# Up projection of two token groups as seven products of half sums, with the first query tiles moved into the key/value stage

## The chip, the cores and the metric

The kernel runs on one core of a Trainium2 chip. Times are device microseconds of one execution on that core. A core has TensorE (PE) for matrix products into PSUM, VectorE (DVE), ScalarE (ACT) and GpSimd (POOL) for work on the elements, and SyncE (SP), which here only issues DMAs. Each engine takes its own instructions strictly in the order in which the program lists them; semaphores make one engine wait for another.

## The reference

One block of a model over 2048 tokens of width 512. After a layernorm, two branches read the same normalised `xn`, and their outputs are added to `x`:

```python
qkv = (x @ wqkv)...                      # 32 heads of 16
pq = einsum("bhsd,hdf->bhsf", q, w_phi); pk = ... k
phi = concat([softmax(p), softmax(-p)])  # 32 features a head
kv = einsum("bhsf,bhsd->bhfd", phi_k, v);  z = sum over s of phi_k
o = (phi_q @ kv) / (phi_q @ z + 1e-6);     A = o @ wo
g = xn @ w_gate;  u = xn @ w_up            # 512 x 1792
B = (g * u) @ w_down
return x + A + B
```

Inputs and output are bf16. The branch B is called the FF branch here; its 1792 columns are 14 "FF tiles" of 128.

## The kernel before

**Layout.** Tokens are 16 tiles of 128, and four groups of 512 (`sg` 0 to 3). `xnT` holds the transposed normalised tokens as four 128-row parts `q`. FF results `h = g*u` lie transposed in `hT`, f16, one 128-row tile for each `ft`.

**How the order comes about.** The code records steps (`sc.step`, `sc.dma`) in a written order, with the memory each step reads and writes; `_record` (line 101) derives the dependencies, for PSUM by whole banks of 512 f32 columns. `_plan` (line 199) then orders the steps on each engine by estimated costs: among the steps that are ready within a small window, the one recorded first goes first. `sc.chain` adds order by hand. The emitted program has a fixed order for each engine and a semaphore wait for every dependency not already known to be met. In `_record`, before the change, a step that overwrites what the same engine (ACT or DVE) only reads needs no wait.

**Stages.**
- Start: ten `warm` products, layernorm of tiles 0 to 3 on DVE, their transposes on PE (`T`, line 597), and FF tiles 0 to 3 for group 0 in small pieces (`U1`, `U2`). An ACT or DVE step copies each transposed tile out of PSUM.
- K/V stage (loop at line 957), once for each token tile: `LN` for later tiles, `K(t)` (line 659), `V(t)` (line 669), and `KV(t)` (line 685), which accumulates in banks 6 and 7. `features` (line 640) makes the projection folded with `w_phi`, two exponentials on ACT, and a reduction (1024 to 64) on DVE; a reciprocal of the sums on DVE follows, then `even_up` on POOL (a ratio and a product of 512 elements). `LN` hands a normalised tile to a DMA transpose on SP. `FOLD` makes the folded weights. Between these, FF units `U(ft, sg)` (line 708) are strewn in: four gate matmuls of 512 columns, copied by ACT into a ring of four slots, four up matmuls, and on DVE the product of both. PSUM tiles of K, V and the FF units come from a ring of six banks.
- Down stage (loop at line 999), in eight pairs of token tiles: `Q(t)` (line 746, like K, then a DMA transpose of `phi_q`), `NUM(t)` (line 764: products with `kv`, division, DMA transpose into `oT`), the down projection, and the FF units left over (line 935 to 937: group 1 and 2 in `U`, group 3 in `U2` of 256 columns). Four banks are left to the ring; banks 4 and 5 serve the down projection.

**The seven products of the down projection.** `DOWN_STEPS` (line 838) already computes each 2 by 2 block product (two token tiles by two column halves, with the 14 FF tiles as two halves of seven) as seven products instead of eight. `TSUMS` and `SSUMS` (lines 804 and 813) make the half sums on POOL; partial results are added in PSUM or by DVE.

Names used below: `nm` is the normalised tile, `xe` the eviction of a transposed tile, `ge`/`ke`/`qe` the ACT evictions of gate, K and Q tiles, `fe` those of the fold, `kr`/`qr` the DVE reductions, `kc`/`qc` the reciprocals, `vs`/`vz` the two steps that scale V by the reciprocal (DVE) and copy the reciprocal (ACT), `h` the DVE product of gate and up, `gu` an FF unit that has both in one bank.

Of the kernel before, what the change touches and what calls it, by code (L numbers as in the profile page):

```python
# [6 lines left out]
F16 = mybir.dt.float16  # L7
# [13 lines left out]
NT = S_TOK // 128  # L21
# [66 lines left out]
class _Sched:  # L88
# [12 lines left out]
    def _record(self, st, reads, writes):  # L101
        deps = []

        def spans(ap):
            space = str(ap.tensor.name)
            ivs = _ap_intervals(ap)
            if space == "ps":
                ivs = sorted(set((b * 2048, b * 2048 + 2048)
                                 for lo, hi in ivs for b in range(lo // 2048, (hi + 2047) // 2048)))
            return space, ivs  # L110

        for ap in reads:
            space, ivs = spans(ap)
            for lo, hi in ivs:
                regs = self._overlaps(space, lo, hi)
                for reg in regs:
                    for w in reg[2]:
                        if w is not st:
                            deps.append(w)
                    if space == "ps":  # L120
                        for r in reg[3]:
                            if r.eng != st.eng:
                                deps.append(r)
                    reg[3].append(st)
                if not regs:
                    raise RuntimeError(f"step {st.idx} ({st.eng} {st.name}) reads unwritten {space}[{lo}:{hi}]")
        for ap in writes:
            space, ivs = spans(ap)
            for lo, hi in ivs:
                new_regions = []  # L130
                for reg in self._overlaps(space, lo, hi):
                    for w in reg[2]:
                        if w is not st:
                            deps.append(w)
                    for r in reg[3]:
                        if r is not st and not (r.eng == st.eng and st.eng in (ACT, DVE)):
                            deps.append(r)
                    if reg[0] < lo:
                        new_regions.append([reg[0], lo, list(reg[2]), list(reg[3])])
                    if reg[1] > hi:  # L140
                        new_regions.append([hi, reg[1], list(reg[2]), list(reg[3])])
                    self.regions[space].remove(reg)
                self.regions[space].extend(new_regions)
                self.regions[space].append([lo, hi, [st], []])
        seen = set()
        dd = []
        for d in deps:
            if id(d) not in seen:
                seen.add(id(d))
                dd.append(d)  # L150
        st.deps = dd
# [192 lines left out]
        _build(nc, es, A_x, A_wqkv, A_w_phi, A_wo, B_w_gate, B_w_up, B_w_down, out)  # L344


def _build(nc, es, A_x, A_wqkv, A_w_phi, A_wo, B_w_gate, B_w_up, B_w_down, out):
    layout = {}
    cur = [0]

    def alloc(name, nelem_bf16):
        off = (cur[0] + 31) // 32 * 32
        layout[name] = off
        cur[0] = off + nelem_bf16
        return off
# [17 lines left out]
    alloc("mask68", 68)  # L373
    alloc("vext", 4 * 8 * 68)
    alloc("E", NE * 1024)
    alloc("qT", NQT * 1024)
    alloc("kvbd", 8 * 68)
    alloc("oring", 3 * 512)
    alloc("oT", 4 * 512)
    alloc("gring", 4 * 512)  # L380
    alloc("hT", NF * 1536)
    alloc("Tw", 3 * 7 * 256)
    alloc("tf", 2 * 2 * 3 * 256)
    alloc("ostg", 4 * 512)
    alloc("stats", 2 * NT * 6)
    alloc("mv", 2 * NT * 2)
    alloc("rstd", 2 * NT)
# [56 lines left out]
    def mm_cost(n):  # L444
        return max(25.0, n / 2.4 + 2.5)

    def mm(items, name=""):
        def fn(e):
            ins = None
            for (o, l, r, s, p) in items:  # L450
                ins = e.matmul(o, lhsT=l, rhs=r, start=s, stop=p, skip_group_check=True)  # L451
            return ins
        reads, writes, c = [], [], 0.0
        for o, l, r, s, p in items:
            reads += [l, r]
            writes.append(o)
            c += mm_cost(o.free_size())
        st = sc.step(PE, fn, reads=reads, writes=writes, cost=c, name=name)
        st.ns = tuple(o.free_size() for o, _, _, _, _ in items)
        return st  # L460
# [159 lines left out]
    def FOLD(w):  # L620
        for dt in range(NQ):
            b = nb()
            mm([(bank(b, jt * 128, 128), wT_v[:, w, jt, dt * 128:(dt + 1) * 128], wbd_v[:, jt, :], True, True)
                for jt in range(NQ)], name=f"F{w}")
            act_op(Wp_v[:, w, dt, :], bank(b), name=f"fe{w}{dt}")

# [24 lines left out]
    def even_up(ev, sm, rc, ratio, name, t):  # L651
# [4 lines left out]
                                       in1=ratio[:, :, None].to_broadcast([128, H, 16]), op=ALU.mult),  # L656
             [ev[:, :, 1, :], ratio], [ev[:, :, 1, :]], 1030.0, name=f"{name}p{t}")

    def K(t):
        Et = Eslot(ectr[0])  # L660
        ectr[0] += 1
        Ek[t] = Et
        sm, rs, ratio = sums_v[:, t % 4, :], rs_v[:, t % 4, :], ratio_v[:, t % 4, :]
        ev = features(Et, 1, t, sm, "k")
        dve(lambda e: e.reciprocal(out=rs, in_=sm), [sm], [rs], cost=500.0, name=f"kc{t}")  # L665
        rv = rs.rearrange("p (h s) -> p h s", s=2)
        even_up(ev, sm, rv[:, :, 1], ratio, "k", t)

# [23 lines left out]
    def KVX():  # L692
        src = psum[:, 6 * 512:8 * 512].rearrange("p (c j) -> p c j", c=8)[:, :, 0:68]
        dve(lambda e: e.tensor_tensor(out=kvbd_v, in0=src, in1=mask68[:, None, :].to_broadcast([128, 8, 68]),
                                      op=ALU.mult), [src, mask68], [kvbd_v], cost=640.0, name="kvx")

    hT_v = sbv("hT", 0, NF * 1536).bitcast(F16).rearrange("p (f s) -> p f s", f=NF)

    def hs(s_lo):
# [8 lines left out]
    def U(ft, sg):  # L708
        bg, bu = nb(), nb()
        s_lo = sg * 512  # L710
        mm(group(bank(bg), [(wg_v[:, q, ft * 128:(ft + 1) * 128], xnT(q, s_lo, 512)) for q in range(NQ)]),
           name=f"g{ft}.{sg}")
        g = gring()
        act_op(g, bank(bg), name=f"ge{ft}.{sg}")
        mm(group(bank(bu), [(wu_v[:, q, ft * 128:(ft + 1) * 128], xnT(q, s_lo, 512)) for q in range(NQ)]),
           name=f"u{ft}.{sg}")
        h = hT_v[:, ft, hs(s_lo):hs(s_lo) + 512]
        dve(lambda e: e.tensor_tensor(out=h, in0=bank(bu), in1=g, op=ALU.mult), [bank(bu), g], [h],  # L718
            name=f"h{ft}.{sg}")

    def U2(ft, s_lo):
        b = nb()
# [23 lines left out]
    def Q(t):  # L746
# [3 lines left out]
        rc = qsm_v[:, t % 4, :]  # L750
        ev = features(Et, 0, t, sm, "q")
        smv = sm.rearrange("p (h s) -> p h s", s=2)
        dve(lambda e: e.reciprocal(out=rc, in_=smv[:, :, 1]), [sm], [rc], cost=270.0, name=f"qc{t}")  # L753
        even_up(ev, sm, rc, ratio, "q", t)
        sc.dma(SP, qT_v[:, t % NQT, :, :], Et, 262144, turn=True, reads=[Et], writes=[qT_v[:, t % NQT, :, :]],
               name=f"qT{t}")
# [33 lines left out]
    S_v = arena[:, so:so + 8 * HF * 128].bitcast(F16).rearrange("p (r w k s) -> p r w k s", r=2, w=4, k=HF)  # L790
    tf_v = sbf("tf", 0, 2 * 3 * 256).rearrange("p (r w j) -> p r w j", r=2, w=3)

    def parts(v):
        return [v[:, k, :] for k in range(v.shape[1])]

    def sums(eng, out_, a_, b_, op, name):
        fn = lambda e: e.tensor_tensor(out=out_, in0=a_, in1=b_, op=op)  # L797
        n = out_.free_size()
        if eng == POOL:
            pool(fn, parts(a_) + parts(b_), parts(out_), 100.0 + 2.0 * n, name=name)  # L800
        else:
            dve(fn, parts(a_) + parts(b_), parts(out_), cost=60.0 + 0.53 * n, name=name)

    def TSUMS():
        for n, (o_, a_, b_) in enumerate(((T1, B12, B11), (T2, B22, T1), (T4, B21, T2), (T3, B22, B12))):
            for lo, hi in ((0, 2), (2, 4), (4, 6), (6, HF)):
# [4 lines left out]
        return hT_v[:, half * HF:(half + 1) * HF, s:s + 128]  # L811

    def SSUMS(p):
        assert ui[0] >= done_by[p]
        S1, S2, S3, S4 = (S_v[:, p % 2, w] for w in range(4))
        A11, A12, A21, A22 = hA(0, 2 * p), hA(1, 2 * p), hA(0, 2 * p + 1), hA(1, 2 * p + 1)
        sums(POOL, S3, A11, A21, ALU.subtract, f"S3.{p}")
# [113 lines left out]
    U2(2, 256)  # L931
    U2(3, 256)
    sc.chain("st0 ag0 st1 ag1 nm0.0 nm0.1 nm1 xe1d st2 ag2 h0t0 st3 ag3 nm2 h1t0 nm3 xe2d xe3d h0t1")
    sc.chain("ln0 rs0 ln1 rs1 xe0a xe0b xe1a ge0t0 ln2 rs2 ge1t0 ln3 rs3 xe2a xe3a")
    units = [(U, ft, 0) for ft in range(4, NF)] + [(U, ft, sg) for sg in (1, 2) for ft in range(NF)]
    done_by = {0: 10, 1: 10, 2: 24, 3: 24, 4: 38, 5: 38, 6: 52, 7: 66}
    units += [(U2, ft, s_lo) for s_lo in (1536, 1792) for ft in range(NF)]
    ui = [0]

    def nextU():  # L940
        if ui[0] < len(units):
            u = units[ui[0]]
            u[0](*u[1:])
            ui[0] += 1

# [5 lines left out]
    nextU()  # L951
    LN([4, 5])
    LN([6, 7])
    NA = 30
    QL = 3
    load_wT(0)
    for t in range(NT):
        if t % 2 == 0 and t + 8 < NT:
            LN([t + 8, t + 9])
        K(t)  # L960
        nextU()
        if t >= 1:
            V(t - 1)
        while ui[0] < 3 + (t + 1) * (NA - 7) / NT:
            nextU()
        if t >= 3:
            KV(t - 3)
        if t == 8:
            FOLD(0)
    sc.dma(SP, wd_v, B_w_down.rearrange("(f p) j -> p f j", p=128), 1835008, writes=[wd_v], name="wd")  # L970
    load_sq(SP, wo_v, A_wo.rearrange("(q p) j -> p q j", p=128), 524288, "wo")
    sc.chain("x12 xT4 xT5 xT6 xT7 wT0 xT8 xT9 xT10 xT11 wd xT12 xT13 wo xT14 xT15")
    TSUMS()
    Q(0)
    V(NT - 1)
    KV(NT - 3)
    nextU()
    Q(1)
    KV(NT - 2)
    nextU()  # L980
    Q(2)
    KV(NT - 1)
    KVX()
    ring_banks[0] = [0, 1, 2, 3]
    rp[0] = 0
    SSUMS(0)
    down = DOWN_STEPS(0)
    nextU()
    Q(3)
    down[0]()  # L990
    down[1]()
    NUM(0)
    nextU()
    NUM(1)
    SSUMS(1)
    u0 = ui[0]
    n_left = len(units) - u0
    NP = NT // 2
    for p in range(NP):
# [29 lines left out]
        down[6]()  # L1029
        some(1.0)  # L1030
        down[7]()

    eng_sems = {e: es.enter_context(nc.semaphore(f"sem_{e}")) for e in (PE, ACT, DVE, POOL, SP)}
    dma_sems = [es.enter_context(nc.semaphore(f"dsem{i}")) for i in range(sc.dma_count)]
# [37 lines left out]
```

## Time and profile before

| | us |
|---|---|
| median of 5 runs (lowest to highest) | 217.81 (217.54 to 218.5) |
| the profiled execution | 217.76 |
| its span, first to last instruction | 215.9 |

The profile is a record of every instruction of one execution. Its page gives the busy time of each engine, the busy share in 40 equal slices of the span, the chain of work that ended last, and groups of instructions by source line. PE is the matmul part of TensorE and PEld its weight loads, which overlap the matmuls. Line 451 is the helper through which every matmul but the warm-up goes, and line 423 the one of most ACT steps, so groups there mix stages; the shapes tell them apart. The mean duration of a PE matmul [...] is longer than the distance from one matmul to the next. Busy shares over the whole span mix stages; the trace can also be asked for the busy time within a window, for what an engine waited for, and for the instructions in order of time.

POOL and DVE are the next busiest by the page, and their load differs by stage:

```profile
DVE  4766599986757756878893747766876588667663
ACT  4656988784464454445343232342142332331000
POOL 4020153459999998285835536839759568322540
```

### The profile page before, as it was taken

The page shows a single profiled execution, that of the slowest core. Times are in us where ns is not written, and L with a number is a line of the kernel's source. Part 1 is how long each engine was busy: PE and PEld are TensorE (multiplying, and loading weights), DVE is VectorE, ACT ScalarE, POOL GpSimd, SP SyncE. Part 2 cuts the span into 40 slices and gives each one's busy share as a digit, 9 for nine tenths or more (in the row PEclk, how much of TensorE's full clock was granted, in tenths as well). Part 3 has the DMA queues.
Part 4 walks back from the last instruction along what each step waited for, and adds up shares of the span by engine and source line. Part 5 has one row for each costly group of instructions (what it writes and reads, how often), then busy time and mean ns, then how long its engine had stood idle before and what let it go on. Part 6 is the DMA issues. An engine that isn't in the chain of part 4 may idle for free.

```text
span 215.9 us, 4165 instructions
## 1 busy us (share of the span) xinstructions
PE 210.6 (98%) x1632; PEld 140.5 (65%) x1654; DVE 152.3 (71%) x313; ACT 91.6 (42%) x204; POOL 123.2 (57%) x143
## 2 busy tenths in 40 slices
PE   8999999999999999999999999999999999999995
PEld 3775444444455444545556667888888889888984
DVE  4766599986757756878893747766876588667663
ACT  4656988784464454445343232342142332331000
POOL 4020153459999998285835536839759568322540
PEclk9999999999999999999999999999999999999999
DMA  5999796792000000003453132162433415434121
GB/s 167 325 262 362 202 105 120 221 290 52 0 0 0 3 0 0 3 0 58 88 102 73 49 76 46 53 100 56 68 73 72 92 34 101 98 73 99 47 78 51
DMA packets 48660, 19.96 MB, mean 92 GB/s; under 512 B 37376, under 2 KB 48640, under 8 KB 48640
## 3 DMA queue, kind: packets, MB, share of 16 engines
q1 hardware_dynamic: 47968, 19.36, 38.8%
q10 hardware_dynamic: 672, 0.33, 0.5%
q8 instruction: 13, 0.21, 0.4%
q14 instruction: 7, 0.06, 0.1%
HBM read 8.67 MB, written 2.10 MB: 50 GB/s over the span
## 4 chain that ended last, share of the span: by engine, by line
PE 93%; DMA 2%; SPq 1%; issue 1%; ACT 0%; DVE 0%; DVEq 0%
PE ps L451 93%; DMA arena<-in_B_w_up_dram 2%; SPq L173 1%; ACT arena L423 0%; DVE arena L729 0%; DVE arena L830 0%; DVEq L343 0%; DVE arena L893 0%
## 5 line engine op out<-in xcount | busy, mean ns | idle before, releaser
L451 PE MATMUL ps<-arena 128*128 128x256 bf16 (+4 forms) x1622 | 206.4, 288 | 2.0 <-DMA arena<-in_B_w_up_dram 0.4
L451 PEld LDWEIGHTS ps<-arena 128*128 128x128 bf16 (+1 forms) x1644 | 139.2, 98 | 69.8 <-DVE arena L583 0.9
L423 ACT ACTIVATE arena<-ps 128x512 bf16<-128x512 f32 (+2 forms) x155 | 75.6, 529 | 94.9 <-PE ps L451 94.4
L797 POOL TENSOR_TENSOR arena<-arena 128x896 f16<-128x896 f16 (+2 forms) x48 | 76.3, 1597 | 25.7 <-PE ps L451 16.9
L647 DVE TENSOR_REDUCE arena<-arena 128x64 f32<-128x1024 bf16 x32 | 38.9, 1217 | 23.6 <-ACT arena L423 23.4
L655 POOL TENSOR_TENSOR arena<-arena 128x512 bf16<-128x512 bf16 x32 | 33.7, 1054 | 1.6
L830 DVE TENSOR_TENSOR arena<-ps,arena 128x256 f32<-128x256 f32 (+1 forms) x56 | 23.2, 413 | 11.9 <-PE ps L451 11.8
L718 DVE TENSOR_TENSOR arena<-ps,arena 128x512 f16<-128x512 f32 x38 | 25.8, 678 | 7.5 <-PE ps L451 7.5
L653 POOL TENSOR_TENSOR arena<-arena 128x32 f32<-128x32 f32 x32 | 8.3, 259 | 32.5 <-DVE arena L753 18.7
L729 DVE TENSOR_TENSOR arena<-ps,arena 128x256 f16<-128x256 f32 x32 | 13.3, 414 | 12.0 <-ACT arena L423 12.0
L423 ACT ACTIVATE arena<-arena 128x2 f32<-128x2 f32 (+2 forms) x32 | 14.0, 457 | 3.6 <-POOL arena L573 2.2
L564 DVE BATCH_NORM_STATS2 arena<-arena 128x6 f32<-128x512 bf16 x16 | 10.5, 676 | 2.1 <-DMA arena<-in_A_x_dram 2.0
L573 POOL TENSOR_SCALAR arena<-arena 128x1 f32<-128x1 f32 x12 | 3.0, 266 | 15.1 <-ACT arena L423 15.1
L777 DVE TENSOR_TENSOR arena<-ps,arena 128x512 bf16<-128x512 f32 x16 | 11.0, 686 | 0.3
L676 DVE TENSOR_TENSOR arena<-ps,arena 128x512 bf16<-128x512 f32 x16 | 10.1, 632 | 0.6 <-PE ps L451 0.6
L665 DVE RECIPROCAL arena<-arena 128x64 f32<-128x64 f32 x16 | 8.7, 542 | 0.0
L679 ACT ACTIVATE arena<-arena 128x32 bf16<-128x32 f32 x16 | 3.7, 232 | 9.3 <-DVE arena L665 9.3
L546 POOL TENSOR_TENSOR arena<-arena 128x128 bf16<-128x128 bf16 x4 | 1.6, 424 | 8.8 <-DMA arena<-in_A_w_phi_dram 8.8
L773 DVE RECIPROCAL arena<-arena 128x32 f32<-128x32 f32 x16 | 5.6, 352 | 0.5
L753 DVE RECIPROCAL arena<-arena 128x32 f32<-128x32 f32 x16 | 5.5, 345 | 0.1
L907 PE MATMUL ps<-const-bfloat16-1.0 128*128 128x512 bf16 x10 | 4.4, 626 | 0.8 <-PEq L1057 0.8
L893 DVE TENSOR_TENSOR arena<-ps,arena 128x256 bf16<-128x256 f32 (+1 forms) x9 | 3.4, 385 | 0.0
(18 smaller groups left out, 16.8 us busy)
## 6 DMA issues: line engine op xcount, KB each, us to landing
arena<-in_B_w_down_dram SPq DMA_DIRECT2D x1, 1792.0 KB, 7.7
out_dram<-arena SPq DMA_DIRECT2D x14, 128.0 KB, 2.0
arena<-in_A_x_dram SPq DMA_DIRECT2D x3, 512.0 KB, 9.3
arena<-in_B_w_gate_dram SPq DMA_DIRECT2D x1, 768.0 KB, 8.0
arena<-in_B_w_up_dram SPq DMA_DIRECT2D x1, 768.0 KB, 8.4
arena<-arena SPq DMA_TRANSPOSE x44, 3.1
arena<-in_B_w_gate_dram SPq DMA_DIRECT2D x2, 256.0 KB, 4.6
arena<-in_B_w_gate_dram SPq DMA_DIRECT2D x1, 512.0 KB, 6.3
```

What stands on the lines that cost most here:

```text
L423: return e.activation(out=out_ap, in_=in_ap, func=func, scale=scale, **kw)
L451: ins = e.matmul(o, lhsT=l, rhs=r, start=s, stop=p, skip_group_check=True)
L564: dve(lambda e, t=t: e.bn_stats(stats_v[:, t, :], x_tile(t)), [x_tile(t)], [stats_v[:, t, :]], cost=560.0, name=f"st{t}", win=win)
L647: dve(lambda e: e.tensor_reduce(out=sm, in_=Et.rearrange("p (h f) -> p h f", f=16), axis=AX.X, op=ALU.add), [Et], [sm], cost=1130.0, name= ...
L655: pool(lambda e: e.tensor_tensor(out=ev[:, :, 1, :], in0=ev[:, :, 1, :], in1=ratio[:, :, None].to_broadcast([128, H, 16]), op=ALU.mult), [ ...
L665: dve(lambda e: e.reciprocal(out=rs, in_=sm), [sm], [rs], cost=500.0, name=f"kc{t}")
L676: dve(lambda e: e.tensor_tensor(out=o1, in0=src, in1=rp_[:, :, :, None].to_broadcast([128, 8, 4, 16]), op=ALU.mult), [src, rs_v[:, t % 4, ...
L718: dve(lambda e: e.tensor_tensor(out=h, in0=bank(bu), in1=g, op=ALU.mult), [bank(bu), g], [h], name=f"h{ft}.{sg}")
L729: dve(lambda e: e.tensor_tensor(out=h, in0=bank(b, 256, 256), in1=g, op=ALU.mult), [bank(b, 256, 256), g], [h], name=f"h{ft}.{s_lo}")
L777: dve(lambda e: e.tensor_tensor(out=ov, in0=src, in1=wv4[:, :, :, None].to_broadcast([128, 8, 4, 16]), op=ALU.mult), [src, w], [o], cost=6 ...
L797: fn = lambda e: e.tensor_tensor(out=out_, in0=a_, in1=b_, op=op)
L830: dve(lambda e: e.tensor_tensor(out=out_, in0=in_ps, in1=in_sb, op=ALU.add), [in_ps, in_sb], [out_], cost=328.0, name=f"{name}.{p}")
```

## The change

For FF tiles 0 to 5 and 7 to 12, the up projection of token groups 1 and 2 becomes seven products. A block takes the 2 by 2 arrangement of FF tiles `ft` and `ft+7` by token groups 1 and 2, with the 512-wide contraction as two halves of 256. Each product is two matmuls of 512 columns. `XSUMS` makes four half sums of `xnT` once, on DVE (eight steps of 128x512); `WSUMS` makes four half sums of `w_up` for each block, on POOL (steps of 128x256). Both are f16. Tiles 6 and 13 keep the old unit. Gate products keep their four matmuls, as units `G` of their own.

```diff
+    def XSUMS(eng):
+        X1, X2, X3, X4 = (Tx_v[:, w] for w in range(4))
+        for n, (o_, a_, b_) in enumerate(((X1, xB(0, 2), xB(0, 1)), (X3, xB(1, 2), xB(0, 2)), (X2, xB(1, 2), X1),
+                                          (X4, xB(1, 1), X2))):
+            for k in range(2):
+                sums(eng, o_[:, k:k + 1], a_[:, k:k + 1], b_[:, k:k + 1], ALU.subtract, f"Xs{n}.{k}")
...
+    def WSUMS(ft):
+        S1, S2, S3, S4 = (Su_v[:, ft % NSW, w] for w in range(4))
+        A = lambda i, k: wA(wu_v, i, k, ft)
+        sums(POOL, S3, A(0, 0), A(1, 0), ALU.subtract, f"w3.{ft}")
+        sums(POOL, S1, A(1, 0), A(1, 1), ALU.add, f"w1.{ft}")
+        sums(POOL, S2, S1, A(0, 0), ALU.subtract, f"w2.{ft}")
+        sums(POOL, S4, A(0, 1), S2, ALU.subtract, f"w4.{ft}")
...
+    def BLOCK(ft, banks):
...
+        def p1():
+            xprod(pa, A(0, 0), xB(0, 1), True, f"b1.{ft}")
+            st["c"] = bank(nb())
+            seed(st["c"], pa, f"sd.{ft}")
+
+        def p7():
+            xprod(pb, S3, X3, True, f"b7.{ft}")
+            st["p7"] = snap()
+            act_op(st["p7"], pb, name=f"s7.{ft}")
+
+        def p2():
+            xprod(st["c"], A(0, 1), xB(1, 1), False, f"b2.{ft}")
+            gated(ft, 1, st["c"])
+
+        def p6():
+            xprod(pa, S2, X2, False, f"b6.{ft}")
+            st["u2"] = snap()
+            act_op(st["u2"], pa, name=f"s2.{ft}")
+
+        def p4():
+            xprod(pb, A(1, 1), X4, False, f"b4.{ft}")
+            add(pb, pb, st["u2"], f"a4.{ft}")
+            gated(ft2, 1, pb)
+
+        def p5():
+            xprod(pa, S1, X1, False, f"b5.{ft}")
+            add(pb, pa, st["p7"], f"a5.{ft}")
+            gated(ft2, 2, pb)
+
+        def p3():
+            xprod(pa, S4, xB(1, 2), False, f"b3.{ft}")
+            gated(ft, 2, pa)
```

Banks 0 and 1 (`pa`, `pb`) belong to the blocks; the ring of the K/V stage shrinks from six banks to banks 2 to 5 at that point. `seed` copies the first product by ACT from `pa` into a ring bank, where the second product is then added by matmuls without a start flag; `snap` keeps two intermediate sums in SBUF. For this the fold's start flag is set only on the first of its four products into a bank:

```diff
-            mm([(bank(b, jt * 128, 128), wT_v[:, w, jt, dt * 128:(dt + 1) * 128], wbd_v[:, jt, :], True, True)
+            mm([(bank(b, jt * 128, 128), wT_v[:, w, jt, dt * 128:(dt + 1) * 128], wbd_v[:, jt, :], jt == 0, jt == NQ - 1)
```

The reciprocals of the K and Q sums move from DVE to ACT, as a logarithm and an exponential:

```diff
+    def recip(out_, in_, name):
+        act_op(out_, in_, func=ACTF.Ln, name=name + "l")
+        act_op(out_, out_, func=ACTF.Exp, scale=-1.0, name=name)
...
-        dve(lambda e: e.reciprocal(out=rs, in_=sm), [sm], [rs], cost=500.0, name=f"kc{t}")
+        recip(rs, sm, f"kc{t}")
...
-        dve(lambda e: e.reciprocal(out=rc, in_=smv[:, :, 1]), [sm], [rc], cost=270.0, name=f"qc{t}")
+        recip(rc, smv[:, :, 1], f"qc{t}")
```

A step that overwrites what its own engine reads now always depends on the reader:

```diff
-                        if r is not st and not (r.eng == st.eng and st.eng in (ACT, DVE)):
+                        if r is not st:
```

The order around the K/V stage changes. `LN` of tiles 8 to 11 is recorded ahead of the loop, that of 12 to 15 in rounds 6 and 7; `Q(0)` to `Q(3)` are recorded in rounds 11 to 14; `FOLD(0)` comes in round 5 instead of 8; the FF units are paced by `PACE`, and all blocks are recorded in the K/V stage, so that the down stage is left with tiles 6 and 13 and group 3. At the start, `gu3.0` is chained behind the transposes of tiles 2 and 3. Some buffers change place, so that the blocks' sums and snapshots can use space that only the down stage needs.

```diff
+    sc.chain("T3.1 gu3.0")
...
+QAT = [11, 12, 13, 14]
+NB = 6
+NSW = 2
...
+def PACE(t, n):
+    return 3 + (t + 1) * 7 / 4.0 if t < 4 else min(n, 10 + (t - 3) * (n - 10) / SL)
...
     for t in range(NT):
-        if t % 2 == 0 and t + 8 < NT:
-            LN([t + 8, t + 9])
+        if t in (LN12, LN12 + 1):
+            LN([12 + 2 * (t - LN12), 13 + 2 * (t - LN12)])
+        if t in QAT:
+            Q(QAT.index(t))
         K(t)
         nextU()
         if t >= 1:
             V(t - 1)
-        while ui[0] < 3 + (t + 1) * (NA - 7) / NT:
+        while ui[0] < PACE(t, NA):
             nextU()
-        if t >= 3:
-            KV(t - 3)
-        if t == 8:
+        KVS(t, 3 if t < QAT[0] - 3 else 2)
+        if t == 5:
             FOLD(0)
```

## The prediction

> **What bounds it now.** I read the page's first three parts, then the waits of PE, the chain of waits around the start, and the busy time in three stages. From the page:
>
> ```profile
> span 215.9 us, 4165 instructions
> PE 210.6 (98%) x1632; PEld 140.5 (65%) x1654; DVE 152.3 (71%) x313; ACT 91.6 (42%) x204; POOL 123.2 (57%) x143
> PE   8999999999999999999999999999999999999995
> PEclk9999999999999999999999999999999999999999
> PE 93%; DMA 2%; SPq 1%; issue 1%; ACT 0%; DVE 0%; DVEq 0%
> ```
>
> PE at full clock from the second slice on, and 93% of the chain that ended last. "Busy" is modelled, so the waits must confirm it. All that PE waited for (us, times, longest):
>
> ```profile
> PE ps L907 <- PEq L1057: 0.8, 1, 0.8
> PE ps L451 <- DMA arena<-in_B_w_up_dram: 0.4, 1, 0.4
> PE ps L451 <- ACT arena L423: 0.4, 1, 0.4
> ```
>
> No wait after 11.4 us: the kernel costs what PE issues. The pitch of one matmul comes from ACT's evictions (start, duration), which follow PE's groups:
>
> ```profile
> 13.35 0.28 ACT L423 ACTIVATE arena<-ps 128x128 bf16<-128x128 f32 x1 [0.17 <-PE ps L451]
> 14.22 0.38 ACT L423 ACTIVATE arena<-ps 128x256 bf16<-128x256 f32 x1 [0.60 <-PE ps L451]
> 15.10 0.38 ACT L423 ACTIVATE arena<-ps 128x256 bf16<-128x256 f32 x1 [0.49 <-PE ps L451]
> 15.96 0.60 ACT L423 ACTIVATE arena<-ps 128x512 bf16<-128x512 f32 x1 [0.48 <-PE ps L451]
> 17.69 0.60 ACT L423 ACTIVATE arena<-ps 128x512 bf16<-128x512 f32 x1 [1.13 <-PE ps L451]
> ```
>
> ge4.0 and ge5.0 lie eight 512-column matmuls apart: 1.73/8 = 0.216 us each. Eight of 256 columns take 15.10 - 14.22 = 0.88, 0.110 each. (The page's mean durations of 0.27 to 0.38 us are pipelined and not a cost.)
>
> **What goes.** Per block, four 512x128 up tiles took 4 x 4 = 16 matmuls of 512 columns; seven products of two take 14. Six blocks save 12 x 0.216 = **2.59 us**. Nothing else leaves PE: 24 gate groups, 16 K, 16 V, 16 Q and both folds keep their matmuls. Half sums in f16 cost PE nothing: f16 and bf16 forms of the down products both show 273 ns.
>
> **The start.** The chain "T3.1 gu3.0" puts the transposes of tiles 2, 3 ahead of gu3.0. Before, they came after it, and PE then idled until their evictions:
>
> ```profile
> 8.61 2.37 PE L451 MATMUL ps<-arena 128*128 128x256 bf16 x24 [0.40 <-DMA arena<-in_B_w_up_dram]
> 11.37 0.83 PE L451 MATMUL ps<-arena 128*128 128x128 bf16 x12 [0.39 <-ACT arena L423]
> 9.34 0.40 DVE L583 TENSOR_SCALAR arena<-arena 128x512 bf16<-128x512 bf16 x1
> ```
>
> Now gu2.0 runs 8.61 to 9.48 (eight of 0.110), T2 to 9.71 (128-column pitch 0.056, from evictions 0.445 apart for eight). T3 waits for nm3, which ends on DVE at 9.74 with about 0.1 to pass on: 9.84 to 10.07. gu3.0 ends at 10.94, and under it the evictions finish. gu1t2 starts then, not at 11.37: **0.43 us** gained, 0 if the evictions are late.
>
> **What is added, and its cover.** In three stages (window, length, then busy us of PE, PEld, DVE, ACT, POOL):
>
> ```profile
> 15.00:39.00 24.00, 23.84 (x129) 11.48 (x130) 19.36 (x39) 19.20 (x42) 5.90 (x14) 1.00 0.84 201
> 39.00:100.00 61.00, 60.63 (x392) 30.22 (x398) 45.10 (x69) 33.40 (x74) 49.59 (x57) 1.00 0.18 48
> L423 ACT ACTIVATE arena<-ps 128x512 bf16<-128x512 f32 x110 | 59.5, 596 | 46.1 <-PE ps L451 45.6
> L647 DVE TENSOR_REDUCE arena<-arena 128x64 f32<-128x1024 bf16 x32 | 38.9, 1217 | 23.6 <-ACT arena L423 23.4
> L797 POOL TENSOR_TENSOR arena<-arena 128x256 f16<-128x256 bf16 x4 | 2.7, 668 | 0.0
> ```
>
> The block stage (K(4) to KV(15) in the built order) holds 71.9 us of PE work at these pitches. ACT: 78 PSUM tiles of 512 (24 K, 8 Q, 24 gate, 4 fold, 6 seeds, 12 snapshots) at 59.5/110 = 0.54 make 42.2; 32 small Ln/Exp at 0.25 (the 128x2 row) 8; 13 vz at 0.23 3; LN the rest, 55 of 71.9 (77%; it had 33 of 61). DVE: 17 reductions at 1.22, 14 vs at 0.63, 23 gated products and 12 adds at 0.68, the X sums 3, together 56 (78%). POOL: 16 even-ups (K and Q) at 1.31 = 21, 8 S sums at 1.88 = 15, 16 weight sums at 0.67 = 11, T sums 16.5: 64 (89%). No engine passes PE. The four Q cost PE the same at either place; their four transposes on SP fall between 50 and 99 us, where SP had nothing, and in return the NUMs of the down stage find them landed.
>
> The reciprocals (0.54 and 0.35 on DVE) become two dependent ACT steps of 0.25. That is cover, but ties ACT, in order, to DVE's reductions: behind a waiting Ln stand exps and evictions that free PE's banks, now four instead of six. The wider WAR rule adds self-waits on ACT and DVE; each costs the overlap of two neighbours, 596 - 540 = 0.06, inside the shares above. Two of the block's DVE steps (a5, then h) really use it.
>
> **Where waits can appear.** (1) The eight X sums stand in DVE's queue behind LN, near 38 us, and wait for the transposes of tiles 8 to 11. Before, their issue lasted until 38.4 while DVE hardly idled:
>
> ```profile
> 30.87 7.50 SPq L172 DMA_TRANSPOSE arena<-arena x4
> 36.15 1.27 DVE L564 BATCH_NORM_STATS2 arena<-arena 128x6 f32<-128x512 bf16 x2
> 37.34 0.16 DVE L566 BATCH_NORM_AGGREGATE arena<-arena 128x2 f32<-128x6 f32 x1
> 37.54 1.22 DVE L647 TENSOR_REDUCE arena<-arena 128x64 f32<-128x1024 bf16 x1
> ```
>
> The last one, issued at 37.1, landed 2.5 us later, at 39.6. LN(8) to LN(11) now come ahead of K(0), some 2 us sooner: 37.6, about when DVE arrives. What does a sum cost? The nearest two-input row (one input in PSUM) says 0.68: 5.4 for eight. [...] the only 16-bit SBUF-to-SBUF row, TENSOR_SCALAR of 512, took 0.41. [...] No DVE row of before has two large SBUF inputs[...]. Five K reciprocals before that point free 5 x 0.46 = 2.3 (their spacing). [...] Behind the sums wait kr3, kr4, vs3 and, through vs3's bank, gate group g7.2 on PE. How much slack DVE had is not shown, only that PE never waited on it: [...] I take **0.5**.
>
> (2) Within a block PE writes bank pa again only after ACT (seed, snapshot) and DVE (a5, h) have read it: four hand-overs per block, 24 in all, each with at least one 0.43 us product or a 0.86 us group of other work in between. With ACT and DVE under 80% and gate groups in the gaps I take **0.2** in all, bounds 0 and 24 x 0.15 = 3.6 (rival D). (3) P4.0 needs oT1 and now follows NUM(1) by only P6, two U2, n2, q5 and P5 on PE: 0.77 + 2 x 0.88 + 0.25 + 0.86 + 0.77 = 4.4 us, against NUM's DVE chain of 1.3 (107.96 to 109.25) and 2.3 to 3.1 to land: 3.6 to 4.4. **0.1**, at most 0.5. The end (S2.7, oT15, last stores) keeps order and distances.
>
> The seed: [...] PE pays nothing; no row of before shows such a seed.
>
> **Sum** against the profiled execution, 217.76 us (span 215.9 and 1.86 around it): 217.76 - 2.59 - 0.43 + 0.5 + 0.2 + 0.1 = **215.5 us**. The median of the runs, 217.81, differs by 0.05. Without any stall it is 214.7.
>
> **Rivals.** B: DVE falls behind at the X sums ([...] the row's price), and PE stalls 1.8 us instead of 0.5: 216.8. For it, DVE's 9.97 of 10 us busy between 30 and 40; against it, banks that bridge a late reader. C: POOL, at 89% the fullest helper, falls behind; a late even-up holds a KV, a late S2 or S4 a product, and PE loses half of the 2.6 us: 217.76 - 1.3 - 0.43 + 0.8 = 216.8 too. Against it, weight sums run two blocks ahead and KV lags K by two or three tiles. D, the slower side: the hand-overs through ACT. If half of the 24 find one 0.54 us eviction ahead of them in ACT's queue, PE loses 12 x 0.54 = 6.5: 217.76 - 3.02 + 6.5 = 221.2. It decides once the mean hand-over is late by over (3.02 + 0.65)/24 = 0.15 us. For it: four ring banks, and ACT behind DVE's reductions; against it: ACT's 23% idle. E: the saving isn't there, because seeds need PE or the products run slower in mixed types: about 217.8.
>
> **Chances.** A change under 0.3% (0.65 us) can't be told from none. Forecast 0.68 (its own range 214.7 to 216.2); B 0.14 and C 0.08, each mostly under the bound of 217.1; D 0.06; E 0.04. Faster: 0.68 + 0.12 + 0.07 = 0.87; same: 0.03 + 0.04 = 0.07; slower: 0.06. The range holds forecast, B and most of C: 214.6 to 217.0; below 214.6 there is only PE's bare work.
>
> **What would show it.** Right: twelve fewer 512-column matmuls, PE without idle from 11 us on, gu1t2 at 10.9; [...] ACT near 77% and POOL near 89% between K(4) and KV(15). Wrong: PE waits on DVE near 45 us (B), on POOL (C) or on ACT's seeds and snapshots (D), or a start at 11.4.

## The result and the profile after

| | before | after |
|---|---|---|
| median (lowest to highest) | 217.88 us (217.37 to 219.72, 51 runs) | 216.69 us (215.51 to 218.81, 30 runs) |
| ratio to before | | 0.9931, 95% interval 0.9919 to 0.9944 |
| profiled execution, its span | 217.76, 215.9 us | 217.05, 215.1 us |

The change is 0.7% faster, about 1.2 us by the medians, where 2.3 were forecast (215.5). In some executions the granted clock was 0.992 instead of 1.00 and the time 1 to 2 us longer (one of the 30 here, 13 of 22 in e3_no_sums, 6 of 14 in g2), so the medians of those two say less than their profiles, which were taken at 1.00. The page of the changed kernel, its span, engines, PE's row and the chain of waits:

```profile
span 215.1 us, 4228 instructions
PE 208.2 (97%) x1619; PEld 139.1 (65%) x1642; DVE 153.5 (71%) x301; ACT 113.2 (53%) x286; POOL 138.3 (64%) x167
PE   8899999979999999999999999999999999999995
PE 82%; ACT 5%; DVE 5%; DMA 4%; issue 1%; POOL 1%; SPq 1%; DVEq 0%
```

PE's row has a 7 in the ninth slice (43 to 48 us), and PE's share of the chain that ended last has gone from 93% to 82%: the chain now runs through DVE, ACT and POOL for a stretch. What PE waited for (us, times, longest):

```profile
PE ps L482 <- DVE arena L712: 1.5, 1, 1.5
PE ps L1038 <- PEq L1210: 0.8, 1, 0.8
PE ps L482 <- DMA arena<-in_B_w_up_dram: 0.6, 1, 0.6
PE ps L482 <- issue: 0.2, 1, 0.2
```

Line 482 is now the matmul helper, and 712 is `vs`. The old wait of 0.4 on ACT, at 11.4 us, is gone. A new one of 1.5 has come. The timeline of PE has it, behind the wait of gu2.0 for its weights (start, duration, idle before and its releaser):

```profile
9.13 35.99 PE L482 MATMUL ps<-arena 128*128 128x256 bf16 x232 [0.57 <-DMA arena<-in_B_w_up_dram]
46.67 165.93 PE L482 MATMUL ps<-arena 128*128 128x512 bf16 x1337 [1.54 <-DVE arena L712]
```

From gu2.0 at 9.13 PE runs without a listed wait to 45.13, waits 1.54 for vs3, and then works to 212.60. DVE ahead of that (line 737 is the helper of all half sums, 596 the layernorm statistics, 679 the reduction, 765 `h` of a unit; the first line at 712 is vs2, the second vs3):

```profile
37.92 0.66 DVE L596 BATCH_NORM_STATS2 arena<-arena 128x6 f32<-128x512 bf16 x1
38.86 0.43 DVE L737 TENSOR_TENSOR arena<-arena 128x512 f16<-128x512 bf16 x1 [0.28 <-DMA arena<-arena]
39.20 1.21 DVE L679 TENSOR_REDUCE arena<-arena 128x64 f32<-128x1024 bf16 x1
40.33 0.68 DVE L765 TENSOR_TENSOR arena<-ps,arena 128x512 f16<-128x512 f32 x1
40.93 0.68 DVE L712 TENSOR_TENSOR arena<-ps,arena 128x512 bf16<-128x512 f32 x1
41.52 2.35 DVE L737 TENSOR_TENSOR arena<-arena 128x512 f16<-128x512 bf16 x4
43.80 1.21 DVE L679 TENSOR_REDUCE arena<-arena 128x64 f32<-128x1024 bf16 x1
44.93 1.08 DVE L737 TENSOR_TENSOR arena<-arena 128x512 f16<-128x512 bf16 x3
45.93 0.68 DVE L712 TENSOR_TENSOR arena<-ps,arena 128x512 bf16<-128x512 f32 x1
```

The first sum waited 0.28 for a transpose that landed at 38.8. Three sums in the last group take 1.08, a spacing of 0.335 (0.414 for one alone). The four from 41.52 on take 2.35, about 0.93 more than four such steps in a row (0.414 + 3 x 0.335 = 1.42). And vs3, for which PE's g7.2 waits, stands behind all eight. It begins 3.4 later than in the kernel before:

```profile
42.52 0.63 DVE L676 TENSOR_TENSOR arena<-ps,arena 128x512 bf16<-128x512 f32 x1
```

The sums are not all that was added ahead of it. The statistics step at 37.92 is the last of all 16; in the kernel before only 14 of the 16 stand ahead of vs3, the last two come at 43.07 and 44.34. POOL at the same time (L685 and L687 are the ratio and the even-up product of K(3)):

```profile
41.64 0.43 POOL L685 TENSOR_TENSOR arena<-arena 128x32 f32<-128x32 f32 x1 [1.99 <-ACT arena L437]
42.14 1.12 POOL L687 TENSOR_TENSOR arena<-arena 128x512 bf16<-128x512 bf16 x1
```

kp3 lies inside the slow four. The block stage by the busy times (window, length, then busy us of PE, PEld, DVE, ACT, POOL):

```profile
39.00:112.00 73.00, 71.04 (x438) 34.65 (x444) 55.16 (x76) 53.40 (x132) 62.93 (x78) 1.00 0.22 55
```

ACT is at 73%, DVE at 76% and POOL at 86% of it, and PE waits for none of them but in that one place.

**The sum of the two profiles.** PE's time from gu2.0 to its last matmul is 204.85 us before (8.61 to 11.37 + 202.09) and 203.47 after. Less the waits (0.39 and 1.54) it is 204.46 and 201.93: 2.53 less. But gu2.0 itself began 0.52 later, because its weights landed later. So 217.76 - 2.53 - 0.39 + 0.52 + 1.54 = 216.90; the last 0.15 to 217.05 lie behind the last matmul and outside the span.

### The profile page after: what moved, and what is told of

It reads as the page before. It is cut to its first block, busy times and chain, and to the rows that moved or that the text cites. A ratio compares the mean times of both kernels' runs of the same rounds, so it can differ in the third digit from the quotient of the medians.

```text
span 215.1 us, 4228 instructions
## 1 busy us (share of the span) xinstructions
PE 208.2 (97%) x1619; PEld 139.1 (65%) x1642; DVE 153.5 (71%) x301; ACT 113.2 (53%) x286; POOL 138.3 (64%) x167
## 4 chain that ended last, share of the span: by engine, by line
PE 82%; ACT 5%; DVE 5%; DMA 4%; issue 1%; POOL 1%; SPq 1%; DVEq 0%
PE ps L482 82%; ACT arena L437 5%; DMA arena<-in_B_w_up_dram 3%; DVE arena L679 2%; DVE arena L737 2%; DMA arena<-arena 1%; SPq L173 1%; DVE arena L712 1%; POOL arena L687 0%; POOL arena L605 0%; DVE arena L765 0%; POOL arena L685 0%; DVE arena L871 0%; DVE arena L961 0%; DVE arena L1024 0%
## 5 line engine op out<-in xcount | busy, mean ns | idle before, releaser
L482 PE MATMUL ps<-arena 128*128 128x256 bf16 (+5 forms) x1609 | 204.0, 287 | 3.6 <-DVE arena L712 1.5
L482 PEld LDWEIGHTS ps<-arena 128*128 128x128 bf16 (+1 forms) x1632 | 137.8, 98 | 70.3 <-DVE arena L712 2.2
L437 ACT ACTIVATE arena<-ps 128x512 bf16<-128x512 f32 (+3 forms) x167 | 83.1, 534 | 73.1 <-PE ps L482 69.2
L737 POOL TENSOR_TENSOR arena<-arena 128x896 f16<-128x896 f16 (+3 forms) x72 | 92.1, 1294 | 24.2 <-PE ps L482 18.8
L679 DVE TENSOR_REDUCE arena<-arena 128x64 f32<-128x1024 bf16 x32 | 38.8, 1215 | 14.1 <-ACT arena L437 14.1
L437 ACT ACTIVATE arena<-arena 128x32 f32<-128x32 f32 (+4 forms) x96 | 28.9, 313 | 11.8 <-DVE arena L679 8.7
L687 POOL TENSOR_TENSOR arena<-arena 128x512 bf16<-128x512 bf16 x32 | 33.9, 1062 | 1.2
L685 POOL TENSOR_TENSOR arena<-arena 128x32 f32<-128x32 f32 x32 | 8.6, 271 | 23.5 <-ACT arena L437 23.5
L813 DVE TENSOR_TENSOR arena<-ps,arena 128x512 f16<-128x512 f32 x24 | 16.3, 686 | 7.5 <-PE ps L482 7.2
L712 DVE TENSOR_TENSOR arena<-ps,arena 128x512 bf16<-128x512 f32 x16 | 10.9, 682 | 2.0 <-PE ps L482 1.4
L919 DVE TENSOR_TENSOR arena<-ps,arena 128x512 bf16<-128x512 f32 x16 | 11.0, 689 | 0.4
L819 DVE TENSOR_TENSOR ps<-ps,arena 128x512 f32<-128x512 f32 x12 | 8.3, 695 | 3.4 <-PE ps L482 3.3
L915 DVE RECIPROCAL arena<-arena 128x32 f32<-128x32 f32 x16 | 5.6, 349 | 0.4
L737 DVE TENSOR_TENSOR arena<-arena 128x512 f16<-128x512 bf16 x8 | 3.9, 531 | 0.3 <-DMA arena<-arena 0.3
```

Source lines behind the costliest of these rows:

```text
L437: return e.activation(out=out_ap, in_=in_ap, func=func, scale=scale, **kw)
L679: dve(lambda e: e.tensor_reduce(out=sm, in_=Et.rearrange("p (h f) -> p h f", f=16), axis=AX.X, op=ALU.add), [Et], [sm], cost=1130.0, name= ...
L687: pool(lambda e: e.tensor_tensor(out=ev[:, :, 1, :], in0=ev[:, :, 1, :], in1=ratio[:, :, None].to_broadcast([128, H, 16]), op=ALU.mult), [ ...
L712: dve(lambda e: e.tensor_tensor(out=o1, in0=src, in1=rp_[:, :, :, None].to_broadcast([128, 8, 4, 16]), op=ALU.mult), [src, rs_v[:, t % 4, ...
L813: dve(lambda e: e.tensor_tensor(out=h, in0=src, in1=g, op=ALU.mult), [src, g], [h], name=f"h{ft}.{sg}")
L919: dve(lambda e: e.tensor_tensor(out=ov, in0=src, in1=wv4[:, :, :, None].to_broadcast([128, 8, 4, 16]), op=ALU.mult), [src, w], [o], cost=6 ...
```

## Experiments

All are variants of the changed kernel but f1_before; times are medians, ratios are to the kernel before, which had a median of 217.86 to 217.95 beside them.

### e1_sums_after: the order of the sums

```diff
+    sc.chain("kr3 Xs0.0 Xs0.1 Xs1.0 Xs1.1 vs3 Xs2.0 Xs2.1 Xs3.0 Xs3.1")
+    sc.chain("k5 g7.2")
```

> The changed kernel, with only the order of DVE's queue altered near 38 to 46 us (two added order constraints): the reduction kr3 goes ahead of the first X sum, and the scaled V of tile 3 (vs3) ahead of the last four X sums. PE's order is as in the changed kernel. Theory 1 (vs3 comes too late because of the X sums in front of it, and PE waits 1.5 us for its bank before gate group g7.2): that wait goes, PE does not wait again at the blocks' first products, and the time falls by 1.0 to 1.5 us against the changed kernel, to some 215.3, with runs closer together. Theory 2 (DVE is simply overloaded up to 46 us and the lateness only moves to the next reader): PE waits 1 us or more at a later place, and the time stays at 216.2 or above. Theory 3 (the shortfall is spread over many small waits on ACT): no difference of over 0.3 us.

Measured: 216.38 us, ratio 0.9924 (0.9895 to 0.9952). The wait on vs3 is gone, and DVE's sums were fast: four in 1.42. But the timeline of DVE, then POOL, then PE in this run shows what came for it:

```profile
40.72 1.42 DVE L737 TENSOR_TENSOR arena<-arena 128x512 f16<-128x512 bf16 x4
```

```profile
40.84 1.43 POOL L685 TENSOR_TENSOR arena<-arena 128x32 f32<-128x32 f32 x1 [1.46 <-ACT arena L437]
```

```profile
52.47 159.36 PE L482 MATMUL ps<-arena 128*128 128x128 bf16 x1310 [0.90 <-ACT arena L437]
```

This time POOL lost: kq3, a ratio of 32 columns that takes 0.27 us elsewhere, took 1.43, as long as the sums beside it. And PE has a new wait of 0.90 before the fold: its bank is freed by ge8.1 on ACT, which stands behind nm14 and nm15 of the layernorm, and nm14 waited for POOL's nb14, which stands behind a half sum S1.0 of 1.88 us:

```profile
49.33 0.81 ACT L437 ACTIVATE arena<-arena 128x512 bf16<-128x512 bf16 x1 [0.55 <-POOL arena L605]
```

That is 0.55 of the 0.90; nm15 waited for nothing. So the order was a cost, but its removal uncovered the next late step.

### e4_no_kp3: one even-up product left out

```diff
+        if name == "k" and t == 3:
+            return
         pool(lambda e: e.tensor_tensor(out=ev[:, :, 1, :], in0=ev[:, :, 1, :],
```

K(3)'s second half of features keeps its value from before the even-up.

> The changed kernel without one POOL instruction, the 512-element product of the even-up of key tile 3 (so tile 3's second half of features stays unscaled); every queue keeps its order. In the changed kernel that product ran 42.1 to 43.3 us, while four X sums on DVE from 41.5 took 2.3 us instead of 4 x 0.33. If an X sum (two SBUF inputs) and a GpSimd operation lock each other out: the four sums take 1.4 us, vs3 is 0.9 us sooner, PE's wait falls from 1.5 to some 0.6 us, and the time by 0.6 to 0.9. If the four sums are slow for another reason (waits on their predecessors, the transposes' traffic): they still take 2.3 us and nothing changes.

Measured: 215.83 us, ratio 0.9907 (0.9886 to 0.9929). DVE and PE:

```profile
41.50 1.49 DVE L739 TENSOR_TENSOR arena<-arena 128x512 f16<-128x512 bf16 x4
```

```profile
45.78 165.94 PE L482 MATMUL ps<-arena 128*128 128x512 bf16 x1356 [0.76 <-DVE arena L714]
```

The same four sums, at the same time, in 1.49 instead of 2.35, and PE's wait halves from 1.54 to 0.76. One POOL instruction of 1.1 us cost half of the stall. The other half stays as long as the sums and the rest of DVE's steps stand ahead of vs3; g3 below moves the sums away.

### e3_no_sums and f2_no_sums_late: no sums on DVE

Both set the X tiles to zero on POOL instead of computing the sums, so the four products of each block that read them (b4 to b7; the second expectation counts five) are left without their input: the first at the start (3 to 7 us), the second at 16 to 20 us.

```diff
-        for n, (o_, a_, b_) in enumerate(((X1, ...
-                sums(eng, o_[:, k:k + 1], ...
+        for n, w in enumerate((0, 2, 1, 3)):
+            pool(lambda e, w=w: e.memset(Tx_v[:, w], 0.0), ..., name=f"Xs{n}")
...
+    sc.chain("w4.0 Xs0 Xs1 Xs2 Xs3")      # f2_no_sums_late alone
```

> The changed kernel without its X sums: the four X tiles are filled with zeros by POOL near the start, where POOL is idle, so part of the up projection is left out. DVE then has neither the eight sums nor the wait for the transposes of tiles 8 to 11. Theory 1 (the X sums cost the 1.5 us wait, and nothing else in the block stage does): 215.2 to 215.4. Theory 3 (waits on ACT, POOL or the four-bank ring hold PE anyway): 216.3 or more. It gives the bound of what any other placing of the sums can gain.

Measured: 217.69 us, ratio 0.9981 (0.9967 to 0.9996): two us above what was expected. The memsets stood beside the layernorm of the first tiles. DVE's normalising steps (L615) in e3_no_sums, POOL's memsets, and the same DVE steps in f2_no_sums_late:

```profile
4.59 2.54 DVE L615 TENSOR_SCALAR arena<-arena 128x256 bf16<-128x256 bf16 x3
```

```profile
3.94 2.73 POOL L783 MEMSET arena<- 128x1024 f16 x3
```

```profile
4.62 1.09 DVE L615 TENSOR_SCALAR arena<-arena 128x256 bf16<-128x256 bf16 x3
```

Three DVE steps took 2.54 instead of 1.09, and PE waited 1.9 us for them at the start. That is not all of the loss: the two profiled executions (217.85 here, 214.94 in f2_no_sums_late) differ by 2.9, of which the longer waits make about 1.4. The rest lies before 13 us, where PE's groups followed each other more slowly than in f2_no_sums_late (two evictions behind them are 1.48 apart instead of 0.90); why is not shown. So three DVE steps with one 16-bit input were slowed here beside POOL steps that only write.

> As e3_no_sums the eight X sums are not made on DVE and the X tiles are zeros, so that the five products of a block that read them give zeros or less than they should; but GpSimd writes the zeros at about 17 to 21 us, not at the start, where DVE makes the layernorm. Theory (e3_no_sums lost at the start what it gained at the sums): no wait of PE on DVE before 16 us beyond that of the kernel before, none at the sums; 215.0 to 215.4 us, the floor of any placing of the sums. Rival (what e3_no_sums lost has nothing to do with where the memsets stand): 217.7 again.

Measured: 215.11 us (214.94 to 215.78, four executions), ratio 0.9873 (0.9854 to 0.9893), as expected. PE:

```profile
8.57 201.86 PE L482 MATMUL ps<-arena 128*128 128x256 bf16 x1569 [0.50 <-DMA arena<-in_B_w_up_dram]
```

From gu2.0 to the last matmul PE has no listed wait: 201.86 us. This is the floor for the rest of the change. The changed kernel's 203.47 over the same stretch lies 1.61 above it, and its stall is 1.54; the medians, 216.69 and 215.11, differ by 1.58. So the sums on DVE are the whole of what is missing.

### e5_no_chain: the start without its constraint

```diff
-    sc.chain("T3.1 gu3.0")
```

> The changed kernel without the constraint that puts the transposes of tiles 2 and 3 ahead of gu3.0. If my sum of the start was right, 0.4 us is lost (PE idles again until the evictions of the transposed tiles). In the profiles of both kernels the eviction ge4.0 began at the same 15.95 us, but the up weights landed 0.5 us later in the changed kernel's; if the constraint brought nothing and that was why, there is no difference. The rest of the kernel is nearly unchanged, so the X sums' wait is in both.

Measured: 217.5 us, ratio 0.9983 (0.9967 to 1.0). PE's timeline has the idle time of the kernel before again:

```profile
9.18 2.37 PE L482 MATMUL ps<-arena 128*128 128x256 bf16 x24 [0.57 <-DMA arena<-in_B_w_up_dram]
11.94 33.77 PE L482 MATMUL ps<-arena 128*128 128x128 bf16 x212 [0.39 <-ACT arena L437]
```

So the chain is worth 0.39 in the profile. The median is 0.8 above the changed kernel's, more than the profile accounts for; the rest stays open.

### f1_before: a second profile of the kernel before

> The kernel before, unchanged, for a second profile of its start. In its first profile w_up's part for gu2.0 landed 5.3 us after its issue and PE's third stretch began at 8.61; in the profiles of the changed kernel and of three of the four variants it was 5.7 to 5.9 and 8.95 to 9.18. If the landing varies from run to run whatever the kernel, about 5.7 (start at about 9.0) is as likely here as 5.3. If the changed kernel makes it later, 5.3 (8.6) again. Time 217.9 either way.

Measured: 217.87 us. Its start:

```profile
9.09 2.37 PE L451 MATMUL ps<-arena 128*128 128x256 bf16 x24 [0.48 <-DMA arena<-in_B_w_up_dram]
11.85 201.93 PE L451 MATMUL ps<-arena 128*128 128x128 bf16 x1558 [0.39 <-ACT arena L423]
```

Here the weights landed 5.8 us after their issue instead of 5.3, and gu2.0 began at 9.09, not 8.61, in the same kernel. Over the twelve profiles in which gu2.0 starts a stretch it began between 8.55 and 9.52, for both kernels. So a difference of 0.52 as in the sum above comes from run to run, without the change.

### f3_order: the next late step moved too

```diff
+    sc.chain("nb15 S1.0")      # on top of e1_sums_after
```

> e1_sums_after with one more order: on POOL the small step nb15 ahead of the half sum S1.0, so that nm15 on ACT, and the gate eviction ge8.1 behind it, are not held by 1.9 us of POOL. Theory (both waits are only misplaced steps of in-order engines, and PE is the bound once they are gone): no PE wait over 0.2 us after 16 us, profiled span about 213.2 to 213.5, 215.2 to 215.5 us, some 1.0 to 1.4 below the changed kernel. Rival 1 (there is always a next step that is late, because POOL is full from 50 to 90 us): S1.0 comes back later and holds something else, a new PE wait of 0.5 us or more on POOL or ACT, and the time stays at that of e1_sums_after, 216.4. Rival 2 (the cost of the changed kernel isn't in these waits): within 0.3 us of the changed kernel, 216.7.

Measured: 216.13 us, ratio 0.9915 (0.989 to 0.994), nearest to rival 1, though the waits are on ACT behind DVE and not on POOL (the profiled execution, 217.08, is the slowest of the six). DVE, ACT and PE:

```profile
40.55 2.36 DVE L737 TENSOR_TENSOR arena<-arena 128x512 f16<-128x512 bf16 x4
```

```profile
46.17 0.30 ACT L437 ACTIVATE arena<-arena 128x2 f32<-128x2 f32 x1 [0.35 <-DVE arena L598]
```

```profile
47.98 4.12 PE L482 MATMUL ps<-arena 128*128 128x512 bf16 x34 [0.53 <-ACT arena L437]
52.78 7.56 PE L482 MATMUL ps<-arena 128*128 128x128 bf16 x43 [0.69 <-ACT arena L437]
```

With DVE's order that of e1_sums_after, the four sums took 2.36 in this run and 1.42 in that one, and POOL's kq3 0.43 instead of 1.43, though it began about 0.1 after the first sum in both (40.66 and 40.55 here, 40.84 and 40.72 there): which of the two engines was held differs between the two, and what decided it is not shown. The late sums delayed a small layernorm step on DVE (ag15, 45.97 instead of 45.13), ACT waited 0.35 for it with ln14, and behind that stood the evictions that PE needed. The second wait, 0.69, is on ge8.1 again, behind nm14 and nm15, though these now waited for nothing. Moving single steps gained little (0.3 us in e1_sums_after and 0.6 here, by the medians) while the sums stood in that place.

### e6_recip_dve: the reciprocals back on DVE

```diff
-        act_op(out_, in_, func=ACTF.Ln, name=name + "l")
-        act_op(out_, out_, func=ACTF.Exp, scale=-1.0, name=name)
+        dve(lambda e: e.reciprocal(out=out_, in_=in_), [in_], [out_], ..., name=name)
```

> The reciprocals of the K and Q sums back on DVE; all else as in the changed kernel. Theory (DVE is late at the X sums): five K reciprocals of 0.46 more on DVE ahead of gate group g7.2's bank, so the stall there grows from 1.5 to 3 us or more, 217.8 to 218.6 us. Rival 1 (the reciprocals on ACT tie ACT to DVE and cost PE hand-overs): PE's other small losses go, and the time is equal to the changed kernel's, 216.7, or below it. Rival 2 (DVE has idle time ahead of the sums that takes the reciprocals up): stall unchanged, 216.5 to 216.9.

Measured: 216.94 us, ratio 0.9969 (0.9949 to 0.999). DVE's first sums and PE:

```profile
38.14 0.76 DVE L736 TENSOR_TENSOR arena<-arena 128x512 f16<-128x512 bf16 x2 [0.77 <-DMA arena<-arena]
```

```profile
46.73 1.25 DVE L596 BATCH_NORM_STATS2 arena<-arena 128x6 f32<-128x512 bf16 x2
```

```profile
46.78 165.88 PE L482 MATMUL ps<-arena 128*128 128x512 bf16 x1335 [1.75 <-DVE arena L711]
```

The stall is 1.75, not 3, and the time is nearest to rival 2, but idle time did not take the reciprocals up: from the first K reduction to vs3 DVE idled 0.96 us here and 0.57 in the changed kernel. The planner, given the reciprocals' cost, ordered DVE anew. Ahead of vs3 stand five reciprocals more (5 x 0.46 = 2.3 us) but three statistics steps and three aggregates of the layernorm fewer (about 2.0 us by their spacing); two of the three steps now come at 46.73, behind vs3, where the changed kernel has all 16 done by 38.6. So more than the reciprocals differs in this run, and what their move is worth with the rest of the order kept is not shown. Without its stall PE's stretch is 202.23 here and 201.93 in the changed kernel, so nothing speaks for rival 1.

### g1, g2: the sums behind kr4, where DVE is idle

In f2_no_sums_late DVE idles from 43.3 to 47.3.

```diff
+    sc.chain("vs3 kr4 Xs0.0 Xs0.1 Xs1.0 Xs1.1 Xs2.0 Xs2.1 Xs3.0 Xs3.1")
+    sc.chain("fe03 ln14")      # g2 alone
```

> All eight X sums moved behind kr4 in DVE's order (vs3, kr4, then the sums), where DVE otherwise had about 4 us of idle time: the floor variant f2_no_sums_late shows it idle from 43.3 to 47.3. kp3 on POOL (about 41 to 42) is over by then, xT11 has long landed, and nothing that PE waits for stands behind the sums before kr5. Theory (the sums cost only because of where they stand): no X-sum wait of PE, four sums in about 1.4 us, at most one more lock against kp4 in the second four; 215.1 to 215.6 us, within 0.5 of the floor 215.11. Rival 1 (the next late step: ge8.1 on ACT behind nm14 and nm15, as in e1_sums_after and f3_order): a PE wait of 0.5 to 0.9 on ACT near 50 us, 215.8 to 216.2. Rival 2 (the sums' own work, not their place, is what costs): b7.0 or b6.0 now waits for them, 1 us or more, 216.4 or above.

> g1, and the layernorm steps of tiles 14 and 15 on ACT (ln14, rs14, nm14, nm15) moved behind the evictions of the fold (fe03), so that neither DVE nor POOL holds ACT through them while block 0 and the fold hand over their banks. Theory: if g1 still has a wait on ACT near 50 us, it is gone here, and the time is at the floor, 215.0 to 215.3; if g1 has none, the same as g1 within 0.2. Rival: the moved steps meet POOL's full stretch from 50 us on, nm14 waits for nb14 behind a T sum of 1.1 us, and holds ge8.2 or ke7 on ACT: a PE wait of 0.3 to 1 us at 55 to 58 us, and no gain over g1.

Measured: g1 216.16 us, ratio 0.9913 (0.9899 to 0.9928); g2 218.25 us, from 216.11 to 219.44 (217.31 for the eight executions with the granted clock at 1.00), ratio 0.9996 (0.9967 to 1.0025). Neither came out as expected. In g1, DVE, POOL and PE:

```profile
43.32 5.38 DVE L737 TENSOR_TENSOR arena<-arena 128x512 f16<-128x512 bf16 x8
```

```profile
45.27 1.12 POOL L687 TENSOR_TENSOR arena<-arena 128x512 bf16<-128x512 bf16 x1
46.35 5.09 POOL L737 TENSOR_TENSOR arena<-arena 128x896 f16<-128x896 f16 x4
```

```profile
51.08 160.60 PE L482 MATMUL ps<-arena 128*128 128x128 bf16 x1305 [0.89 <-DVE arena L813]
```

The eight sums took 5.38 instead of 2.7, beside kp4 and then S1.0; one of them alone took 2.10. The reduction kr5 came late, with it vs4 and h0.1 (L813), and PE waited for h0.1. In g2 they took 6.36 and PE waited 1.87 in the same place.

### g3: the same place with POOL held

```diff
     SSUMS(0)
+    sc.chain("kp4 S1.0")
+    by_name = {st.name: st for st in sc.steps}
+    by_name["kq4"].deps.append(by_name["Xs3.1"])
```

> g1 with one semaphore more: on POOL, the small ratio kq4, and with it the even-up product kp4 and all that follows in POOL's order, waits until the last X sum is done on DVE; S1.0 goes behind kp4. DVE then has 2.7 us for the sums with nothing on POOL beside them. Theory (in g1 and g2 the eight sums took 5.4 and 6.4 us instead of 2.7 only because kp4 and the half sums of POOL ran beside them): the eight sums in 2.7 to 2.9 us, kr5 no longer late, no PE wait between 16 and 60 us, span 212.9 to 213.3 and 215.0 to 215.4 us: the floor 215.11, below both kernels, with the sums made. Rival 1 (the sums are slow behind kr4 for another reason): 5 us again and 216.2. Rival 2 (POOL, held for 1 to 2 us ahead of its full stretch, is now late for a product or a KV): a PE wait on POOL after 50 us, 215.6 to 216.3.

Measured: **215.33 us** (215.1 to 215.79, four executions), ratio 0.9878 (0.9859 to 0.9898). DVE, POOL and PE:

```profile
44.13 2.76 DVE L737 TENSOR_TENSOR arena<-arena 128x512 f16<-128x512 bf16 x8
```

```profile
46.97 0.27 POOL L685 TENSOR_TENSOR arena<-arena 128x32 f32<-128x32 f32 x1 [2.87 <-DVE arena L737]
```

```profile
9.52 201.84 PE L482 MATMUL ps<-arena 128*128 128x256 bf16 x1569 [0.52 <-DMA arena<-in_B_w_up_dram]
```

POOL waits 2.87 us (1.47 in g1, where it waited for ACT), the sums take 2.76, and PE has no listed wait from gu2.0 to the end: 201.84, the floor. POOL made up for the wait without PE noticing. g3 computes everything and is faster than both kernels, 1.4 us below the changed one by the medians. The eight sums (shortest, median and longest ns of one) in the changed kernel, g1 and g3:

```profile
L737 DVE TENSOR_TENSOR arena<-arena x8: 408/414/1273, 38.9 to 45.6; 128x512 f16<-128x512 bf16 x8
```

```profile
L737 DVE TENSOR_TENSOR arena<-arena x8: 416/418/2100, 43.3 to 46.6; 128x512 f16<-128x512 bf16 x8
```

```profile
L737 DVE TENSOR_TENSOR arena<-arena x8: 412/414/417, 44.1 to 46.5; 128x512 f16<-128x512 bf16 x8
```

The median does not move; the longest ones make the difference.

## Why the prediction was right or wrong

The direction, the place of the risk and the range (214.6 to 217.0) held. The forecast's 215.5 did not: its stall was a third of the real one. Rival B (216.8, DVE behind at the X sums with 1.8 us of stall) describes the result better than the likeliest case did, and the range held because it was drawn to take in B.

1. **Twelve matmuls, 2.59 us: right.** The floor's 201.86 against 204.46 for the kernel before (its 204.85 less 0.39) is 2.60; against the second profile of before (204.69 - 0.39) it is 2.44. In the changed kernel and the other variants in which gu2.0 starts a stretch, it is 201.93 to 202.29 less the listed waits, so the saving is 2.0 to 2.6 by the profiles.
2. **The start, 0.43: right in the profile (0.39, e5_no_chain).** In the one profiled run of the changed kernel it can't be seen, because gu2.0's weights landed 0.5 later there, as they did in f1_before.
3. **The stall at the X sums, 0.5: wrong, 1.54.** The 0.5 was the author's estimate: no trace of before showed what such a sum costs, what a POOL step beside it adds, or how much lateness PE's banks could bear. A sum cost 0.335 by its spacing (0.414 alone), half of the row's 0.68, and a POOL product beside them added 0.93 to four (e4_no_kp3, without it, has them 0.86 shorter). At the row's price eight sums would have taken 5.4, and less the 2.3 of the five K reciprocals DVE would have ended 3.1 later. Measured, vs3 began 3.4 later (45.93 instead of 42.52), from other parts. The 2.3 did leave DVE, but two statistics steps of the layernorm moved up into the place (about 1.2 with an aggregate), which the prediction did not have. And the last transpose, put at 37.6, landed at 38.8, so that DVE, which in the kernel before had no listed idle time from its first K reduction to vs3, idled 0.57, half of it for that transpose. So 3.6 (8 x 0.335 and 0.93) - 2.3 + 1.2 + 0.6 makes 3.1 of the 3.4. PE felt 1.54 of it; that its banks bridged some of the rest was rightly expected, but not how much.
4. **Hand-overs through ACT, 0.2, and P4.0, 0.1: nothing to be seen.** PE's stretch in f2_no_sums_late and g3 is 201.86 and 201.84, where 204.46 - 2.59 = 201.87 leaves no room for either; the up to 0.4 more in other variants is not traced. Rival D (221.2) falls with it. That the seeds cost PE nothing was the author's estimate, with no trace of before to show it; the same two stretches leave no room for a cost (one matmul of 0.216 for each of the six would be 1.3 us), so E falls too.
5. **No engine passes PE: right,** with 73, 76 and 86% against 77, 78 and 89. POOL's even-up had its part in the stall, but not by being late (rival C): the four sums beside it took 2.35, and 1.49 without it. No run shows PE waiting for POOL itself.

The sum with the measured terms, 217.76 - 2.60 - 0.39 + 1.54, is 216.3; with the late start (0.52) and the tail (0.15) of the profiled run it is 217.0, against the 217.05 of that run.

## What to carry to other kernels

Before placing a DVE step with two SBUF inputs, lay POOL's queue beside it: here four such steps took 2.35 us beside a POOL product of 1.12, and 1.49 without it, and the cure was to make POOL wait (2.87 us in g3, with all eight in 2.76). Where a planner orders the steps, an edit that takes work off an engine lets other steps move up into its place: count what stands ahead of the critical step in the built order before subtracting the time that was freed. And when one wait is removed, run the kernel again before believing the sum: twice here, the next step that was late took most of it back (PE waited 0.90 us in e1_sums_after and 0.89 in g1, after 1.54).

## What the runs showed of the hardware

- DVE steps with both inputs in SBUF and GpSimd steps slowed each other, and either could lose: the eight sums took 2.76 us in g3 with POOL held, 5.38 in g1 and 6.36 in g2 beside POOL's steps; in e1_sums_after four sums kept their 1.42, and a POOL step that takes 0.27 elsewhere took 1.43.
- Not foreseen: three 16-bit TENSOR_SCALAR steps of DVE took 2.54 us beside GpSimd memsets, which read nothing (e3_no_sums), and 1.09 without them (f2_no_sums_late).
- DVE products with one input in PSUM were not seen to be slowed: the 82 of 128x512 took 0.66 to 0.70 us each in the changed kernel, in g1 and in g3. One of g1's (vs4, at 49.75) took 0.68 while POOL's half sums ran from 46.35 to 51.44.
- The landing of the same weight load took 5.3 us in one profile of the kernel before and 5.8 in the other (f1_before), half a microsecond of the total.
